# Half of the sums of halves in FFN2's seven-product multiplication made by GpSimd instead of VectorE

## The chip, the cores and the metric

The kernel runs on one core of one Trainium2 chip. The metric is the device time of one execution in microseconds (us); lower is better. The core's engines are TensorE (PE in the profile; PEld is its weight load), VectorE (DVE), ScalarE (ACT), GpSimd (POOL) and SyncE (SP). Each runs its own instructions in order, and they wait for one another by semaphores.

## What is computed

Attention without softmax, then a two-layer feed-forward net whose activation has a learned slope for negative values. The core of the reference:

```python
# q, k, v: [8 batches, 12 heads, 448, 64];  d_model = 768, d_ff = 2048
scores = (1 / sqrt(64)) * q @ k.T
attn   = maximum(scores, 0) ** 2 / 448
x      = (attn @ v)                      # -> [8 * 448 = 3584 tokens, 768]
h      = x @ w_in                        # FFN1
g      = maximum(h, 0) + alpha * minimum(h, 0)
out    = g @ w_out                       # FFN2
```

## The kernel before

**Work and order.** Attention goes by quads: a quad is four heads of one batch, 24 quads in all, each in seven chunks (j = 0 to 6). A chunk is four score products on TensorE (L206), a relu that empties their two PSUM banks to `rl` (L215 on ScalarE or L217 on VectorE), and a square to `at` (L226 or L228). When a quad's seven chunks are there, 28 products with `vraw` (L237) make its part of x, and two copies (L249, L251) take that to `xT`. FFN1 goes by batch and by blocks `ff` of 128 hidden features, 16 of them: six matmuls (L303) into one bank, then ScalarE makes `neg` = relu(-h) (L310, L653) and VectorE makes `gT` from it and the bank (L311, L659, L541). FFN2 takes 128 tokens at a time, 28 tiles.

The order on every engine is written out by hand, as strings of words that `Walk` (P[0] to P[3]) and `Line` (P[4]) read. Instructions of one engine stand in its queue in the order of these words. A word `ca` or `cAAD` is chunks, `f` is a block of FFN1, `N` and `G` its `neg` and `gT`, `v` an attention output, `t` and `l` belong to the loads (below), and `+`, `*` and `-` to the pairs of FFN2.

**FFN2 by pairs.** Four tiles of tokens go one by one (L330); the other 24 go in 12 pairs, named a to l. A pair's two tiles and the two halves of the features give four blocks of g, a11 and a12 (first tile) and a21 and a22 (second); likewise w_out has four blocks, of which `w_mix` holds four mixtures (L356). Seven products of eight matmuls (L379) take the place of eight. For them `Pair.mix` makes four sums of halves of g, each 128 x 1024 in bf16:

```python
x, y, op = {1: (self.a21, self.a22, ALU.add),
            2: (self.s.get(1), self.a11, ALU.subtract),
            3: (self.a11, self.a21, ALU.subtract),
            4: (self.a12, self.s.get(2), ALU.subtract)}[i]
nc.vector.tensor_tensor(t, x, y, op)          # L415
```

The words for them end in a, b, c, d for sums 1, 2, 3, 4: `+aa` and `*ba` are sum 1 of pairs a and b. Sum 1 is read by sum 2 and by product 5; sum 2 by product 6 and by sum 4, which is written over it; sum 3 by product 7; sum 4 by product 3. Products 1, 2 and 4 read g itself. The outputs of the products are added up by L396 and L392 (`m`, `u`, `osb`) and stored by SyncE (L320). In the trace sums 1 and 3 read `S<-gT`, sum 2 `S<-S,gT`, sum 4 `S<-gT,S`. The tiles of S come from a pool of four.

**GpSimd's queue.** GpSimd issues the loads: q and k of a quad (L109), v (L116), and the weights. From quad 5 on, q and k are turned by a DMA transpose: a copy to `perm` (L188, L693) by VectorE or ScalarE, then SyncE's DMA_TRANSPOSE (L193) to `T`. Right after that stands `land` (L435), a copy of one element of `T` to `landed` on GpSimd, which so waits until the transpose has arrived; behind it stand the next quads' loads.

Of the kernel before, what the change touches and what calls it, by code (L numbers as in the profile page):

```python
# [20 lines left out]
def kernel(  # L21
# [10 lines left out]
    nc = tc.nc  # L32
# [113 lines left out]
    for lo, hi, eng in ((0, 4, nc.sync), (4, NJ, nc.scalar)):  # L146
        t = o_pool.tile([128, 2, (hi - lo) * D], F32, tag="o", name=f"qfirst{lo}")
# [141 lines left out]
    def may_read(t, halves=(0, 1)):  # L289
        for b in batches_of(*t):  # L290
            for h in halves:
                assert all((b, ff) in f1_done for ff in range(KF // 2 * h, KF // 2 * h + KF // 2)), "gT is not written"
# [65 lines left out]
    class Pair:  # L358
# [43 lines left out]
        def mix(self, *which):  # L402
            for i in which:
                for t, halves in {1: ((self.b, (0, 1)),), 2: ((self.a, (0,)),), 3: ((self.a, (0,)), (self.b, (0,))),
                                  4: ((self.a, (1,)),)}[i]:
                    may_read(t, halves)
                assert i != 4 or "6" in self.made
                self.made.append("abcd"[i - 1])
                t = self.s[2] if i == 4 else S_pool.tile([128, KH, 128], BF16, tag="S", name="S")
                self.s[i] = t  # L410
                x, y, op = {1: (self.a21, self.a22, ALU.add),
                            2: (self.s.get(1), self.a11, ALU.subtract),
                            3: (self.a11, self.a21, ALU.subtract),
                            4: (self.a12, self.s.get(2), ALU.subtract)}[i]
                nc.vector.tensor_tensor(t, x, y, op)  # L415

        def run(self, name):
            if name in "23":
# [392 lines left out]
```

## Time and profile before

| | us |
|---|---|
| median of 2 runs (lowest, highest) | 371.59 (371.26, 371.92) |
| the profiled execution, its own time | 371.61 |
| its span, first to last instruction | 369.5 |
| busy: TensorE / VectorE / ScalarE / GpSimd | 361.2 / 310.9 / 256.3 / 73.0 |
| VectorE's 48 sums (L415) | 32.8, 0.68 each |
| GpSimd's 18 landing copies: busy, and idle ahead of them | 4.8, 182.4 |

How to read it: a row of the list in order of time has a start and a length in us from the span's start, the engine, the line of the kernel, the operation, what it writes and reads, and how many; in brackets how long the engine was idle before it and what ended that. A row of stretches has its limits, its length and then the busy time of each engine with the number of instructions in brackets, the granted TensorE clock as a share of full speed, the share of the DMA engines, and GB/s. The profile counts the issue of a load (0.7 us) as busy time on GpSimd. TensorE's ends are modelled. GpSimd's spans are rough.

### The profile page before, as it was taken

What the parts mean: (1) busy time and instruction counts of PE and PEld (TensorE: products, weight loads), DVE (VectorE), ACT (ScalarE), POOL (GpSimd) and SP (SyncE); (2) the same over time, 40 slices, a digit from 0 to 9 for tenths busy, and PEclk for the clock granted to TensorE, in tenths of its full rate; (3) what the DMA queues carried; (4) which work ended last, traced back from release to release, by engine and by line L of the source; (5) the groups of instructions that cost most, each with busy time, mean ns of one, the idle gap of its engine ahead of it and who ended that gap; (6) DMA issues with size and microseconds to landing.
All of it is one profiled execution on the core that took longest, in us unless ns stands there. A gap on an engine that the chain in (4) does not pass through costs nothing.

```text
span 369.5 us, 8035 instructions
## 1 busy us (share of the span) xinstructions
PE 361.2 (98%) x3169; PEld 201.7 (55%) x3169; DVE 310.9 (84%) x513; ACT 256.3 (69%) x388; POOL 73.0 (20%) x120
## 2 busy tenths in 40 slices
PE   8799999999999999999999999999999999999995
PEld 6454564445454455445554555555555555778763
DVE  3989988885979989999989989898786869789873
ACT  5998676877998878888678778887754834344300
POOL 8567150304122222201231122020000000000000
PEclk9999999999999999999999999999999999999999
DMA  9999989998999858758796675882134110020125
GB/s 141 188 204 202 201 125 190 164 168 138 193 186 154 119 82 149 142 96 110 126 171 122 105 117 105 141 154 52 28 73 105 46 43 2 21 66 23 44 59 134
DMA packets 73398, 43.29 MB, mean 117 GB/s; under 512 B 40336, under 2 KB 72848, under 8 KB 73360
## 3 DMA queue, kind: packets, MB, share of 16 engines
q0 software_dynamic: 27136, 22.58, 41.9%
q1 hardware_dynamic: 45792, 19.81, 26.6%
q8 instruction: 24, 0.39, 0.4%
q10 hardware_dynamic: 432, 0.39, 0.4%
q14 instruction: 14, 0.11, 0.1%
HBM read 45.62 MB, written 11.01 MB: 153 GB/s over the span
## 4 chain that ended last, share of the span: by engine, by line
PE 89%; DVE 3%; ACT 3%; DMA 2%; issue 2%; SPq 1%; ACTq 0%; POOLq 0%
PE psum L303 32%; PE psum L379 28%; PE psum L206 9%; PE psum L237 9%; PE psum L330 6%; PE psum L501 4%; ACT rl L215 1%; DMA kraw<-in_k_dram 1%; DMA out_dram<-osb 1%; DVE gT L311 1%; ACT neg L310 1%; DVE w_mix L188 1%; PE psum L175 1%; SPq L320 1%; DVE T L178 0%
## 5 line engine op out<-in xcount | busy, mean ns | idle before, releaser
L303 PE MATMUL psum<-xT,w_in_sb 128*128 128x448 bf16 x672 | 134.5, 353 | 0.5 <-ACT xT L249 0.3
L215 ACT ACTIVATE rl<-psum 128x896 bf16<-128x896 f32 x114 | 100.9, 929 | 20.0 <-PE psum L206 15.9
L303 PEld LDWEIGHTS <-w_in_sb 128*128 128x128 bf16 x672 | 63.4, 98 | 65.2 <-issue 10.0
L217 DVE TENSOR_SCALAR rl<-psum 128x896 bf16<-128x896 f32 x54 | 58.5, 1086 | 11.3 <-PE psum L206 10.5
L228 DVE TENSOR_TENSOR at<-rl 128x896 bf16<-128x896 bf16 x105 | 61.9, 617 | 1.1 <-ACT rl L215 0.6
L653 ACT ACTIVATE neg<-psum 128x448 f32<-128x448 f32 x80 | 43.1, 547 | 23.7 <-PE psum L303 12.5
L659 DVE SCALAR_TENSOR_TENSOR gT<-neg,beta_sb,psum 128x448 bf16<-128x448 f32 x80 | 53.0, 676 | 7.6 <-ACT neg L653 6.4
L226 ACT ACTIVATE at<-rl 128x896 bf16<-128x896 bf16 x63 | 58.2, 954 | 0.1
L379 PEld LDWEIGHTS <-S 128*128 128x128 bf16 x384 | 36.7, 98 | 26.4 <-issue 3.4
L379 PE MATMUL psum<-w_mix,S 128*128 128x384 bf16 x288 | 51.0, 326 | 0.0
L206 PE MATMUL psum<-T 64*64 64x448 bf16 x672 | 46.5, 357 | 1.7 <-ACT rl L215 0.9
L435 POOL COPY landed<-T 1x1 bf16<-1x1 bf16 x18 | 4.8, 267 | 182.4 <-DMA T<-perm 158.8
L379 PEld LDWEIGHTS <-gT 128*128 128x128 bf16 x288 | 27.6, 98 | 20.0 <-issue 2.5
L237 PE MATMUL psum<-at,vraw 64*64 64x448 bf16 x672 | 36.2, 350 | 0.0
L379 PE MATMUL psum<-w_out_sb,gT 128*128 128x384 bf16 x192 | 34.9, 326 | 0.0
L396 DVE TENSOR_TENSOR osb<-psum,u 128x384 f32<-128x384 f32 x36 | 19.7, 553 | 12.0 <-PE psum L379 7.1
L206 PEld LDWEIGHTS <-T 64*64 64x64 bf16 x672 | 16.8, 105 | 23.1 <-issue 15.8
L237 PEld LDWEIGHTS <-vraw 64*64 64x64 bf16 x672 | 20.1, 107 | 12.5 <-issue 1.7
L311 DVE SCALAR_TENSOR_TENSOR gT<-neg,beta_sb,psum 128x448 bf16<-128x448 f32 x32 | 21.0, 677 | 3.9 <-ACT neg L310 3.3
L310 ACT ACTIVATE neg<-psum 128x448 f32<-128x448 f32 x32 | 17.2, 548 | 8.8 <-PE psum L303 6.1
L330 PE MATMUL psum<-w_out_sb,gT 128*128 128x512 bf16 (+1 forms) x128 | 22.0, 326 | 0.1
L249 ACT ACTIVATE xT<-psum 128x448 bf16<-128x448 f32 x28 | 15.5, 557 | 4.5 <-PE psum L237 4.5
(75 smaller groups left out, 339.3 us busy)
## 6 DMA issues: line engine op xcount, KB each, us to landing
out_dram<-osb SPq DMA_DIRECT2D x94, 96.0 KB, 2.2
vraw<-in_v_dram POOLq DMA_DIRECT2D x24, 224.0 KB, 6.3
qraw<-in_q_dram POOLq DMA_DIRECT2D x23, 224.0 KB, 4.1
kraw<-in_k_dram POOLq DMA_DIRECT2D x23, 224.0 KB, 5.9
w_in_sb<-in_moe_w_in_dram POOLq DMA_DIRECT2D x16, 192.0 KB, 7.9
w_out_sb<-in_moe_w_out_dram POOLq DMA_DIRECT2D x4, 512.0 KB, 10.1
w_out_sb<-in_moe_w_out_dram POOLq DMA_DIRECT2D x4, 256.0 KB, 8.6
out_dram<-osb SPq DMA_DIRECT2D x8, 128.0 KB, 2.9
```

Of the source, the lines that this page charges most:

```text
L206: nc.tensor.matmul(ps[64 * c:64 * c + 64, r, :S], t[64 * r:64 * r + 64, 1, j, 64 * c:64 * c + 64], t[64 * r:64 * r + 64, 0, :, 64 * c:64 * ...
L215: nc.scalar.activation(rl, ps[:, :, :S], ACTF.Relu)
L217: nc.vector.tensor_scalar(rl, ps[:, :, :S], 0.0, None, ALU.max)
L226: nc.scalar.activation(a, rl, ACTF.Square)
L228: nc.vector.tensor_tensor(a, rl, rl, ALU.mult)
L237: nc.tensor.matmul(ps[64 * s:64 * s + 64, r, :S], vv[64 * r:64 * r + 64, s, j, :], a[64 * r:64 * r + 64, s], start=(j == 0), stop=(j == NJ ...
L303: nc.tensor.matmul(ps, w_in_sb[:, km // 2, km % 2, bass.ts(ff, 128)], xT[b][:, km // 2, km % 2, :], start=(km == 0), stop=(km == KM - 1))
L311: nc.vector.scalar_tensor_tensor(gT[:, ff, (b % 2) * S:(b % 2) * S + S], neg, beta_sb[:, ff:ff + 1], ps, ALU.mult, ALU.add)
L330: nc.tensor.matmul(psum[:, i, :hi - lo], gT[:, ff, bass.ts(c, 128)], w_out_sb[:, ff, lo:hi], start=(ff == 0), stop=(ff == KF - 1))
L379: nc.tensor.matmul(ps, left[:, i], right[:, i], start=(start and i == 0), stop=(i == KH - 1), skip_group_check=not start)
L653: nc.scalar.activation(neg, ps, ACTF.Relu, scale=-1.0)
L659: nc.vector.scalar_tensor_tensor(gT[:, ff, (b % 2) * S:(b % 2) * S + S], neg, beta_sb[:, ff:ff + 1], ps, ALU.mult, ALU.add)
```

## The change

Sums 1 and 3 of every pair are made by GpSimd, sums 2 and 4 stay on VectorE. The words of the order are the same, so each of the 24 sums that move takes its place in GpSimd's queue by where its word stands:

```diff
                             2: (self.s.get(1), self.a11, ALU.subtract),
                             3: (self.a11, self.a21, ALU.subtract),
                             4: (self.a12, self.s.get(2), ALU.subtract)}[i]
-                nc.vector.tensor_tensor(t, x, y, op)
+                (nc.gpsimd if i in (1, 3) else nc.vector).tensor_tensor(t, x, y, op)
```

TensorE's and ScalarE's orders stay as they are. Sum 2 now waits for GpSimd's semaphore, and products 5 and 7 too.

GpSimd at the first pair (P[3], words `l9` to `l10`), after the change; before, the sums' row is not there and the rest reads the same. The first landing copy is that of quad 9, the second that of quad 10:

```order
L435 COPY landed<-T 1x1
L109 DMA qraw<-in_q_dram 128x2x448
L109 DMA kraw<-in_k_dram 128x2x448
L116 DMA vraw<-in_v_dram 128x2x448
L415 TENSOR_TENSOR S<-gT 128x1024 x2
L435 COPY landed<-T 1x1
```

Sums 1 and 3 of pair a stand behind quad 9's landing copy and the three loads that follow it.

VectorE at the same place, before:

```order
L356 TENSOR_TENSOR w_mix_101<-w_out_sb 128x1536
L415 TENSOR_TENSOR S<-gT 128x1024
L228 TENSOR_TENSOR at<-rl 128x896
L415 TENSOR_TENSOR S<-gT 128x1024
L415 TENSOR_TENSOR S<-S,gT 128x1024
L228 TENSOR_TENSOR at<-rl 128x896 x2
L356 TENSOR_TENSOR w_mix_101<-w_out_sb 128x1536
L217 TENSOR_SCALAR rl<-psum 128x896
```

and after:

```order
L356 TENSOR_TENSOR w_mix_101<-w_out_sb 128x1536
L228 TENSOR_TENSOR at<-rl 128x896
L415 TENSOR_TENSOR S<-S,gT 128x1024
L228 TENSOR_TENSOR at<-rl 128x896 x2
L356 TENSOR_TENSOR w_mix_101<-w_out_sb 128x1536
L217 TENSOR_SCALAR rl<-psum 128x896
```

Sum 2 keeps its place among the squares, the mixture of w_out and the relu; the two sums ahead of it are gone from this queue.

GpSimd from pair g to the end, after the change:

```order
L435 COPY landed<-T 1x1
L109 DMA qraw<-in_q_dram 128x2x448
L109 DMA kraw<-in_k_dram 128x2x448
L116 DMA vraw<-in_v_dram 128x2x448
L415 TENSOR_TENSOR S<-gT 128x1024 x2
L435 COPY landed<-T 1x1
L116 DMA vraw<-in_v_dram 128x2x448
L435 COPY landed<-T 1x1
L415 TENSOR_TENSOR S<-gT 128x1024 x10
```

Pair g's two sums stand behind the loads of a landing copy, and the ten sums of pairs h to l behind the last one, with nothing else on the queue. In pairs i and j sum 3 of each comes first, and in i to l sum 1 of one pair is followed by sum 1 of its partner.

## The prediction

> **What bounds the kernel now.** I read the page's busy shares and chain first, then TensorE by stretches of the span, then GpSimd, VectorE and TensorE in order of time around the first pair.
>
> ```profile
> PE 361.2 (98%) x3169; PEld 201.7 (55%) x3169; DVE 310.9 (84%) x513; ACT 256.3 (69%) x388; POOL 73.0 (20%) x120
> PE 89%; DVE 3%; ACT 3%; DMA 2%; issue 2%; SPq 1%; ACTq 0%; POOLq 0%
> 92.00:112.00 20.00, 19.75 (x195) 9.91 (x194) 17.40 (x29) 19.41 (x26) 4.52 (x7) 1.00 1.02 181
> 112.00:300.00 188.00, 187.94 (x1618) 98.51 (x1616) 165.59 (x260) 144.91 (x213) 28.95 (x50) 1.00 0.63 109
> 300.00:365.00 65.00, 65.00 (x465) 44.39 (x458) 53.88 (x104) 21.02 (x42) 0.00 (x0) 1.00 0.19 45
> ```
>
> The last three rows are stretches: length, then busy time of PE, PEld, DVE, ACT, POOL. TensorE sets the time: from 92 us, where the sums begin, to 365 it is idle for 0.25 + 0.06 + 0 = 0.3 us. Time taken off VectorE there can buy at most that 0.3, while whatever makes TensorE wait is added to the end. GpSimd's 20% is not free time in the sense that matters, since its queue is in order and spends its idle time inside one waiting instruction, as the next rows show.
>
> **The first pair.** GpSimd, VectorE and TensorE from 87 to 100 us (start, length, instruction):
>
> ```profile
> 87.56 0.75 POOL L116 DMA_DIRECT2D vraw<-in_v_dram  x1
> 99.45 0.84 POOL L435 COPY landed<-T 1x1 bf16<-1x1 bf16 x1 [11.14 <-DMA T<-perm]
> 100.24 0.72 POOL L109 DMA_DIRECT2D qraw<-in_q_dram  x1
> 101.71 0.72 POOL L109 DMA_DIRECT2D kraw<-in_k_dram  x1 [0.75 <-DVE xT L251]
> 102.42 0.72 POOL L116 DMA_DIRECT2D vraw<-in_v_dram  x1
> ```
> ```profile
> 93.37 0.68 DVE L415 TENSOR_TENSOR S<-gT 128x1024 bf16<-128x1024 bf16 x1
> ...
> 95.11 0.68 DVE L415 TENSOR_TENSOR S<-S,gT 128x1024 bf16<-128x1024 bf16 x1
> 95.71 1.28 DVE L228 TENSOR_TENSOR at<-rl 128x896 bf16<-128x896 bf16 x2
> 96.90 0.95 DVE L356 TENSOR_TENSOR w_mix<-w_out_sb 128x1536 bf16<-128x1536 bf16 x1
> 97.77 1.08 DVE L217 TENSOR_SCALAR rl<-psum 128x896 bf16<-128x896 f32 x1
> ...
> 99.31 0.95 DVE L356 TENSOR_TENSOR w_mix<-w_out_sb,w_mix 128x1536 bf16<-128x1536 bf16 x1
> ```
> ```profile
> 97.71 1.66 PE L237 MATMUL psum<-at,vraw 64*64 64x448 bf16 x28
> 99.03 0.72 PE L206 MATMUL psum<-T 64*64 64x448 bf16 x8
> ```
>
> In the changed order the pair's sums 1 and 3 stand on GpSimd behind this landing copy and its three loads. The copy waits for quad 9's transpose, which nothing in the change brings forward, so sum 1 cannot begin before the loads are issued: at 99.45 + 0.18 (the copy undisturbed, below) + 0.3 of issue + 3 x 0.72 = 102.1 at the earliest, at 103.14 if the copy stays long and the 0.75 gap before kraw stays. I take 102.5. Sum 2 (95.11 now) stays on VectorE and reads sum 1. Until it comes, everything behind it on VectorE waits: two squares, a w_mix half, the relu at 97.77.
>
> **What a sum costs on GpSimd.** No GpSimd instruction with two inputs is in the trace. The nearest rows:
>
> ```profile
> 0.31 0.10 POOL L795 MEMSET const-bfloat16-1.0<- 128x1 bf16 x1
> 2.07 0.22 POOL masks.py:197 MEMSET ident<- 128x128 bf16 x1
> 2.37 0.29 POOL masks.py:199 TENSOR_SCALAR_AFFINE_SELECT ident<-ident 128x128 bf16<-128x128 bf16 x1
> L415 DVE TENSOR_TENSOR S<-gT 128x1024 bf16<-128x1024 bf16 x24 | 16.4, 683 | 0.1
> ```
>
> A write costs (0.22 - 0.10) / 127 = 0.95 ns an element, one input raises it to (0.29 - 0.10) / 127 = 1.5. Two inputs, extrapolated: about 2.0 ns x 1024 + 0.10 = 2.1 us. Ends: 1.1 us (the write's slope alone) and 3.2 (two passes at the one-input slope). I take 2.1, as it is nearest to what the rows say of inputs.
>
> [...]
>
> **The terms**, against the profiled execution's own 371.61 us (span 369.5 and 2.1 around it), which stands 0.02 above the median of the runs.
>
> 1. *VectorE held at pair a: 9.1 us.* Sum 1 ends at 102.5 + 2.1 = 104.6, sum 2 starts at 104.65 in place of 95.11: VectorE is 9.5 late. TensorE first lacks a square of the two from 95.71 within the 28 matmuls from 97.71 on, then the bank that the relu (97.77 to 98.85) empties for the second half of the eight from 99.03, some 0.2 into them. So 0.4 of the 9.5 is slack: 9.1 on the path. Ends 7.6 (sum of 1.1 us, start at 102.1) and 10.8 (3.2 us, 103.1).
>
> 2. *TensorE's clock: 2.0 us.* It would sit idle from about 98.8 to 106. What idling does shows at the span's two ends:
>
> ```profile
> 1.06 4.13 PE L157 MATMUL psum<-idle 128*128 128x128 bf16 x37 [1.06 <-DVE idle L143]
> 10.71 0.62 PE L626 MATMUL psum<-idle 128*128 128x128 bf16 x8
> 363.91 1.46 PE L379 MATMUL psum<-w_out_sb,gT 128*128 128x384 bf16 x8
> 365.40:367.80 2.40, 0.00 (x0) 0.00 (x0) 0.00 (x0) 0.48 (x1) 0.00 (x0) 1.00 0.73 191
> 367.90:369.40 1.50, 0.00 (x0) 0.00 (x0) 0.00 (x0) 0.00 (x0) 0.00 (x0) 0.50 0.00 1
> ```
>
> The granted clock falls to 0.50 some 2.5 us after the last matmul (365.37). At the start the same matmul comes every (4.13 - 0.31) / 36 = 0.106 us for 3.8 us (0.31 is one's own length); at 10.7 us every (0.62 - 0.22) / 7 = 0.057. So after 7 idle us about 4 us run at half pace: 2.0 lost. Ends 0 (it stays up) and 3.
>
> 3. *Other sums that come late: 2.2 us.* The same reckoning for all 24, with GpSimd's loads and the inputs' times, leaves these places; the rest end before they are wanted.
>
> ```profile
> 242.53 0.73 POOL L116 DMA_DIRECT2D vraw<-in_v_dram  x1
> 243.59 0.68 DVE L415 TENSOR_TENSOR S<-S,gT 128x1024 bf16<-128x1024 bf16 x1
> 316.13 0.67 DVE L659 SCALAR_TENSOR_TENSOR gT<-neg,beta_sb,psum 128x448 bf16<-128x448 f32 x1
> 317.74 0.69 DVE L415 TENSOR_TENSOR S<-S,gT 128x1024 bf16<-128x1024 bf16 x1
> 318.81 1.17 PEld L379 LDWEIGHTS <-S 128*128 128x128 bf16 x8
> 348.86 1.26 DVE L541 SCALAR_TENSOR_TENSOR gT<-ng,beta_sb,psum 128x448 bf16<-128x448 f32 x2
> 350.89 0.69 DVE L415 TENSOR_TENSOR S<-S,gT 128x1024 bf16<-128x1024 bf16 x1
> 352.05 3.51 PEld L379 LDWEIGHTS <-S 128*128 128x128 bf16 x22
> ```
>
> Pair g: loads end at 243.26, sum 1 at 245.4, sum 2 wanted at 243.59: VectorE 1.8 late; its next works are F1 outputs, so I charge 0.5. Pair i: the last gT lands at 316.8, sum 1 ends at 318.9, sum 2 was to start at 317.74: 1.2 late, and product 6 loads sum 2 at 318.81, 0.38 after its end: 0.8. Pair k: gT at 350.1, sum 1 ends at 352.2 against 350.89: 1.35 late, product 6 loads it 0.47 after its end: 0.9. Ends 0.3 and 5.5.
>
> 4. *Collisions of GpSimd with VectorE: 3.7 us.*
>
> ```profile
> 110.09 0.18 POOL L435 COPY landed<-T 1x1 bf16<-1x1 bf16 x1 [6.95 <-DMA T<-perm]
> 176.72 0.68 DVE L415 TENSOR_TENSOR S<-gT,S 128x1024 bf16<-128x1024 bf16 x1
> 176.87 0.57 POOL L435 COPY landed<-T 1x1 bf16<-1x1 bf16 x1 [9.00 <-DMA T<-perm]
> ```
>
> A landing copy of one element takes 0.18 us. Those begun inside a VectorE instruction with two SBUF inputs last until it ends: 0.57 here (to 177.44 against 177.40), 0.84 at 99.45 (to 100.29, the w_mix above ends at 100.26). The other direction, VectorE held by a 2.1 us GpSimd sum, no row shows: between 0 and 2.1 each. It counts where a GpSimd sum follows at once behind the one that sum 2 awaits and so starts first: pairs a, b, g, i, k (sum 3, or the partner pair's sum 1). At half, about 1.0 each, less what slack is left: 1.0 + 0.2 + 0.7 + 0.9 + 0.9 = 3.7. Ends 0 and 9.
>
> [...]
>
> 5. *VectorE's relief: -0.3.* It loses 24 x 0.6 = 14 us of work, covered by the 0.3 that TensorE is idle.
>
> Moved past and left as it is: each later landing copy stands behind one or two sums, but waits 159 / 16 = 10 us for its transpose anyway, longer than two sums take, so the loads leave on time:
>
> ```profile
> POOL landed L435 <- DMA T<-perm: 158.8, 16, 16.1
> ```
>
> Sum: 9.1 + 2.0 + 2.2 + 3.7 - 0.3 = 16.7; 371.6 + 16.7 = **388.3 us**.
>
> **Rivals.** *Not slower, 371.3 us:* GpSimd makes sum 1 of pair a inside its idle stretch from 88.31 to 99.45 (its gT was ready then), so VectorE is not held and only the relief is left. It decides if the sum starts before about 92. For it: GpSimd idle for 11.14 us. Against it: the order, where the sum stands behind the waiting copy on the same queue. 0.03. *VectorE held for whole sums:* five collisions at full length, 2.1 + 1.0 + 1.8 + 2.1 + 2.1 = 9.1 in place of 3.7: 393.7. For it: the landing copies; against it, only that this direction is unseen. 0.27. *Everything cheap:* a sum of 1.1 us, no clock drop, no collision, 7.6 + 0.3: 379.5. It needs three things at once. 0.09. *A sum of 3.2 us or more:* 10.8 + 2.0 + 5.5 + 5: about 395, and more if it collides whole. 0.06. That the change does nothing is excluded: 24 instructions leave VectorE in the order.
>
> **How the numbers follow.** Forecast 0.55, rivals 0.27, 0.09, 0.06, 0.03. The range 380.5 to 397 leaves out the cheapest end, the longest collisions and the rival of no loss. Slower by over 2% (above 379.0; 2% is about what a measurement of this kernel can tell from no change) is every case but the last and a part of the cheap one: 0.95; within 0.04; faster 0.01.
>
> **What would show it.** Right: L415 on GpSimd x24 at some 2.1 us; its first start near 102.5; an idle VectorE of about 10 us before S<-S,gT at 105, a wait of TensorE on L228 and L217 there, a granted clock of 0.5 for about 4 us; small waits of PEld L379 in the last 60 us. Wrong: a GpSimd sum before 99 us, or a VectorE that goes on past its waiting sum; terms 2 and 4 are wrong if the clock stays at 1.00 or sum 2 starts the moment sum 1 ends while sum 3 runs.

## The result and the profile after

| | us |
|---|---|
| before | 371.59 |
| after, median of 2 runs (lowest, highest) | 405.6 (404.25, 406.95) |
| ratio, with its 95% interval | 1.0911 (1.0886 to 1.0937) |
| after, the profiled execution: its own time, its span | 406.95, 405.2 |

The forecast was 388.3 and its range ended at 397, so the kernel lost about twice what was foreseen. In some experiments below the profiled execution was the slowest of its kernel (whole reads, quarter sums, both remedies together), and three of ten executions of the run with writes took 612 to 2101 us: sizes are taken from the medians, the ratios leave these executions out, and what is read from such a profile holds for that execution.

The page of the kernel after, engines and granted clock:

```profile
PE 370.1 (91%) x3169; PEld 204.2 (50%) x3169; DVE 319.1 (79%) x489; ACT 256.7 (63%) x388; POOL 123.3 (30%) x144
...
PEclk9999999999689999999998999999999999899989
```

VectorE has 24 instructions fewer and is busy 8.2 us longer (319.1 against 310.9): that is the first sign that something else than waiting happens to it. The clock drops at four places, not at one. Its stretches at 0.50, and one between the first two, from the view of stretches (length, busy time of PE, PEld, DVE, ACT, POOL, then the clock):

```profile
103.94:114.18 10.24, 3.72 (x20) 1.55 (x20) 8.34 (x9) 2.77 (x4) 3.93 (x2) 0.50 0.33 47
216.58:219.99 3.41, 3.29 (x11) 1.27 (x10) 3.41 (x6) 2.62 (x4) 0.00 (x0) 0.50 0.25 59
349.70:353.11 3.41, 3.41 (x18) 2.43 (x16) 2.01 (x4) 0.59 (x2) 0.00 (x0) 0.50 0.00 0
387.24:390.65 3.41, 3.41 (x13) 1.57 (x12) 1.79 (x4) 0.00 (x0) 0.00 (x0) 0.50 0.24 58
114.18:216.58 102.40, 95.89 (x844) 49.56 (x842) 91.73 (x128) 76.99 (x114) 36.82 (x41) 1.00 0.71 118
```

The groups of VectorE that matter here, in the kernel before:

```profile
L228 DVE TENSOR_TENSOR at<-rl 128x896 bf16<-128x896 bf16 x105 | 61.9, 617 | 1.1 <-ACT rl L215 0.6
L659 DVE SCALAR_TENSOR_TENSOR gT<-neg,beta_sb,psum 128x448 bf16<-128x448 f32 x80 | 53.0, 676 | 7.6 <-ACT neg L653 6.4
L415 DVE TENSOR_TENSOR S<-S,gT 128x1024 bf16<-128x1024 bf16 x12 | 8.2, 684 | 0.1
L415 DVE TENSOR_TENSOR S<-gT,S 128x1024 bf16<-128x1024 bf16 x12 | 8.2, 682 | 0.0
```

and after, with GpSimd's sums:

```profile
L228 DVE TENSOR_TENSOR at<-rl 128x896 bf16<-128x896 bf16 x105 | 72.2, 717 | 1.7 <-ACT rl L215 1.2
L659 DVE SCALAR_TENSOR_TENSOR gT<-neg,beta_sb,psum 128x448 bf16<-128x448 f32 x80 | 52.9, 675 | 10.2 <-ACT neg L653 9.1
L415 DVE TENSOR_TENSOR S<-S,gT 128x1024 bf16<-128x1024 bf16 x12 | 18.1, 1508 | 20.0 <-POOL S L415 20.0
L415 DVE TENSOR_TENSOR S<-gT,S 128x1024 bf16<-128x1024 bf16 x12 | 9.6, 803 | 0.0
```
```profile
L415 POOL TENSOR_TENSOR S<-gT 128x1024 bf16<-128x1024 bf16 x24 | 51.2, 2152 | 72.7 <-DVE gT L659 39.5
```

A sum takes 2.15 us on GpSimd; the estimate was 2.1. VectorE's instructions with two inputs in SBUF (squares, sums 2, sums 4) grew by 10.3 + 9.9 + 1.4 = 21.6 us, while L659, which reads one of its inputs from PSUM, stayed (53.0 and 52.9). Besides, sum 2 waited 20.0 us for sum 1.

The first pair in order of time:

```profile
99.96 0.18 POOL L435 COPY landed<-T 1x1 bf16<-1x1 bf16 x1 [10.97 <-DMA T<-perm]
...
102.22 0.72 POOL L109 DMA_DIRECT2D kraw<-in_k_dram  x1 [1.02 <-issue]
102.93 0.72 POOL L116 DMA_DIRECT2D vraw<-in_v_dram  x1
103.67 4.20 POOL L415 TENSOR_TENSOR S<-gT 128x1024 bf16<-128x1024 bf16 x2
105.84 2.60 DVE L415 TENSOR_TENSOR S<-S,gT 128x1024 bf16<-128x1024 bf16 x1 [11.44 <-POOL S L415]
108.36 1.15 DVE L228 TENSOR_TENSOR at<-rl 128x896 bf16<-128x896 bf16 x2
109.02 0.59 PE L237 MATMUL psum<-at,vraw 64*64 64x448 bf16 x4 [9.43 <-DVE at L228]
```

The order is the one that the prediction gave: the copy, the loads, sum 1 (at 103.67, it took 102.5), then sum 2, whose 0.68 us became 2.60 while sum 3 ran until 107.87.

TensorE does the same matmuls in the same order in both kernels, so the start of one can be subtracted from the start of the same one. This gives how late TensorE is, and where it becomes late (times of before; the total is 35.7):

| place | what TensorE lacked | predicted | measured |
|---|---|---|---|
| pair a, 98.8 and 99.2 | a square, then a relu | 9.1 + 1.0 = 10.1 | 9.8 + 2.0 = 11.8 |
| pairs i and k, 318.9 and 352.2 | sum 2 | 1.7 + 1.8 = 3.5 | 2.9 + 2.8 = 5.7 |
| pair g, 247.6 and 250.4 | a relu, then gT | 0.5 + 0.7 = 1.2 | 2.1 + 1.3 = 3.4 |
| pairs b, c, d, e, f | work that stands on VectorE behind held squares or a sum 2 (relus, an output, a copy); at b a relu of ScalarE that waits for a held square | 0.2 | 1.7 + 1.9 + 0.7 + 2.8 + 1.0 = 8.1 |
| half clock | | 2.0 | 1.1 + 3 x 1.7 = 6.2 |
| relief | | -0.3 | not seen |

The rows of pairs b to f and of the half clock carry most of the miss: 8.1 us where 0.2 was given, 6.2 where 2.0 was. The rows add up to 35.2; TensorE is 0.4 late already at 92, and the rest is rounding.

Pair c shows what term 3's words "the rest end before they are wanted" left out. Its sums are wanted later, but one of them runs beside a square:

```profile
158.67 0.73 POOL L116 DMA_DIRECT2D vraw<-in_v_dram  x1
...
159.32 2.73 DVE L228 TENSOR_TENSOR at<-rl 128x896 bf16<-128x896 bf16 x1
...
159.40 2.16 POOL L415 TENSOR_TENSOR S<-gT 128x1024 bf16<-128x1024 bf16 x1
...
161.98 1.08 DVE L217 TENSOR_SCALAR rl<-psum 128x896 bf16<-128x896 f32 x1
```

The square lasts until 162.05, 0.49 behind the sum's end, and the relu behind it on VectorE ends at 163.06; TensorE waits for that and loses 1.9. At pair e the loss is larger, since both of the pair's sums follow each other:

```profile
209.33 0.73 POOL L116 DMA_DIRECT2D vraw<-in_v_dram  x1
209.52 5.79 DVE L228 TENSOR_TENSOR at<-rl 128x896 bf16<-128x896 bf16 x2 [1.06 <-ACT rl L215]
210.06 4.23 POOL L415 TENSOR_TENSOR S<-gT 128x1024 bf16<-128x1024 bf16 x2
```

The two squares (1.15 us for two at 108.36) end 1.02 after the second sum: neither came through before it ended.

### The profile page after: what moved, and what is told of

It reads as the page before. It is cut to its first block, busy times and chain, and to the rows that moved or that the text cites. A ratio compares the mean times of both kernels' runs of the same rounds, so it can differ in the third digit from the quotient of the medians.

```text
span 405.2 us, 8043 instructions
## 1 busy us (share of the span) xinstructions
PE 370.1 (91%) x3169; PEld 204.2 (50%) x3169; DVE 319.1 (79%) x489; ACT 256.7 (63%) x388; POOL 123.3 (30%) x144
## 5 line engine op out<-in xcount | busy, mean ns | idle before, releaser
L303 PE MATMUL psum<-xT,w_in_sb 128*128 128x448 bf16 x672 | 136.1, 355 | 5.2 <-ACT rl L215 2.0
L228 DVE TENSOR_TENSOR at<-rl 128x896 bf16<-128x896 bf16 x105 | 72.2, 717 | 1.7 <-ACT rl L215 1.2
L415 POOL TENSOR_TENSOR S<-gT 128x1024 bf16<-128x1024 bf16 x24 | 51.2, 2152 | 72.7 <-DVE gT L659 39.5
L659 DVE SCALAR_TENSOR_TENSOR gT<-neg,beta_sb,psum 128x448 bf16<-128x448 f32 x80 | 52.9, 675 | 10.2 <-ACT neg L653 9.1
L379 PE MATMUL psum<-w_mix,S 128*128 128x384 bf16 x288 | 54.4, 341 | 5.3 <-DVE S L415 5.3
L206 PE MATMUL psum<-T 64*64 64x448 bf16 x672 | 48.7, 360 | 7.7 <-DVE rl L217 3.6
L435 POOL COPY landed<-T 1x1 bf16<-1x1 bf16 x18 | 3.6, 198 | 170.8 <-DMA T<-perm 133.7
L379 PEld LDWEIGHTS <-S 128*128 128x128 bf16 x384 | 37.8, 101 | 34.3 <-issue 6.6
L415 DVE TENSOR_TENSOR S<-S,gT 128x1024 bf16<-128x1024 bf16 x12 | 18.1, 1508 | 20.0 <-POOL S L415 20.0
## 6 DMA issues: line engine op xcount, KB each, us to landing
w_out_sb<-in_moe_w_out_dram POOLq DMA_DIRECT2D x4, 512.0 KB, 10.6
```

The source lines that it names most:

```text
L206: nc.tensor.matmul(ps[64 * c:64 * c + 64, r, :S], t[64 * r:64 * r + 64, 1, j, 64 * c:64 * c + 64], t[64 * r:64 * r + 64, 0, :, 64 * c:64 * ...
L228: nc.vector.tensor_tensor(a, rl, rl, ALU.mult)
L303: nc.tensor.matmul(ps, w_in_sb[:, km // 2, km % 2, bass.ts(ff, 128)], xT[b][:, km // 2, km % 2, :], start=(km == 0), stop=(km == KM - 1))
L379: nc.tensor.matmul(ps, left[:, i], right[:, i], start=(start and i == 0), stop=(i == KH - 1), skip_group_check=not start)
L415: (nc.gpsimd if i in (1, 3) else nc.vector).tensor_tensor(t, x, y, op)
L659: nc.vector.scalar_tensor_tensor(gT[:, ff, (b % 2) * S:(b % 2) * S + S], neg, beta_sb[:, ff:ff + 1], ps, ALU.mult, ALU.add)
```

## The experiments

Two theories were tested. *Exclusion:* while GpSimd reads SBUF for a sum, a VectorE instruction with two SBUF inputs stands still until the sum's end, wherever it is (sum 2 at pair a: 2.60 us in place of 0.68), and this makes most of the loss outside pair a. *Waits:* the loss is sum 2 and the products waiting for sums that come late, and what stands beside them costs nothing. All ratios are to the kernel before on the same chip, with the 95% interval.

### Pair a alone

```diff
-nc.vector.tensor_tensor(t, x, y, op)
+(nc.gpsimd if i in (1, 3) and self.a == (0, 3) else nc.vector).tensor_tensor(t, x, y, op)
```

> Only pair a's sums 1 and 3 go to GpSimd, the other 22 stay on VectorE. In the changed kernel TensorE's delay against before grows by 12.8 us at pair a (from 0.4 at 92 us to 13.2 at 112): 9.7 in the attention product, 2.0 at the relu behind sum 2, 1.0 at half clock. If these 12.8 belong to that place alone, 371.6 + 12.8 = 384.4 us, within 1.5. If instead VectorE without its relief catches up or loses elsewhere, it lies under 381 or over 388.

Measured: 385.49 us, 1.0377 (1.0360 to 1.0394). TensorE is 14.0 late at 112 and stays at that to the end. So pair a is worth 14 us by itself, and 20 of the 34 arise elsewhere, though the forecast had 4.6 there (16.7 less 12.1).

### Readers and writers on GpSimd that nothing waits for

VectorE makes all 48 sums as before; GpSimd repeats sums 1 and 3 into a scratch tile that nobody reads, in four pieces:

```diff
 nc.vector.tensor_tensor(t, x, y, op)
+if i in (1, 3):
+    for c in range(0, KH, 2):
+        nc.gpsimd.tensor_tensor(scratch, x[:, c:c + 2], y[:, c:c + 2], op)
```

> All 48 sums stay on VectorE. GpSimd makes sums 1 and 3 a second time, at the same places of its queue, in four pieces of 256 columns, and throws them away into a small scratch tile. Nothing waits for them. Theory of exclusion (a VectorE instruction with two SBUF inputs can't run while GpSimd reads SBUF, and is held to the end of GpSimd's work): the squares and sums of VectorE still get held, so 380 to 392 us and squares (L228 in the rows of before) above 650 ns on the mean. Theory of waits (all the loss comes from work that waits for a sum that is late): 371 to 373.5 us, squares at 617 ns.

Measured: 374.2 us, 1.0086 (1.0064 to 1.0109). The squares took 654 ns on the mean, as exclusion had it, but the time lies between the two theories. In place of the readers, writers:

```diff
+if i in (1, 3):
+    for c in range(6):
+        nc.gpsimd.memset(scratch, 1.0)
```

> All 48 sums stay on VectorE. GpSimd fills a scratch tile instead, six memsets of 256 columns at each of the same 24 places, about as long (6 x 0.35 = 2.1 us), without reading SBUF. If only reads of GpSimd exclude VectorE's two-input instructions: 371 to 373 us, squares at 617 ns. If any GpSimd instruction does: as the run with extra reads, 380 or more. Theory of waits: 371 to 373.

Measured: 371.54 us, 0.9996 (0.9986 to 1.0006). Groups of the writers' kernel (first fence) and of the readers' (second):

```profile
L419 POOL MEMSET scratch<- 128x256 bf16 x144 | 45.1, 313 | 7.6
L229 DVE TENSOR_TENSOR at<-rl 128x896 bf16<-128x896 bf16 x105 | 62.0, 618 | 1.1 <-ACT rl L216 0.6
L416 DVE TENSOR_TENSOR S<-gT 128x1024 bf16<-128x1024 bf16 x24 | 16.4, 684 | 0.1
```
```profile
L419 POOL TENSOR_TENSOR scratch<-gT 128x256 bf16<-128x256 bf16 x96 | 76.1, 793 | 60.1 <-DVE gT L663 31.8 <-DVE gT L545 22.2
L229 DVE TENSOR_TENSOR at<-rl 128x896 bf16<-128x896 bf16 x105 | 65.7, 654 | 1.0 <-ACT rl L216 0.6
L416 DVE TENSOR_TENSOR S<-gT 128x1024 bf16<-128x1024 bf16 x24 | 18.8, 783 | 0.1
```

45 us of writes leave VectorE's sums at 684 ns and its squares at 618; 76 us of reads lengthen them to 783 and 654. In these two runs it is the reading that holds. Whether the small loss came from the short pieces was then asked with whole ones. To make room for a scratch tile of 1024 columns, the outputs got five buffers instead of six, and a kernel with only that is the control:

```diff
-    o_pool = ctx.enter_context(tc.tile_pool(name="o", bufs=6))
+    o_pool = ctx.enter_context(tc.tile_pool(name="o", bufs=5))
 ...
+if i in (1, 3):
+    nc.gpsimd.tensor_tensor(scratch, x, y, op)
```

> As the run with extra reads, but each thrown-away GpSimd sum is one instruction of 1024 columns, as in the changed kernel (to make room for the scratch tile, the pool of output tiles has five buffers in place of six). No instruction waits for these sums; VectorE makes all 48 itself. Theory of exclusion: VectorE is held for whole GpSimd sums, squares near 700 ns on the mean, 382 to 391 us. Theory of waits: 371 to 373.

> The kernel before with five output buffers in place of six, the control for the run with whole extra reads: 371 to 372.5 us by both theories.

Measured: whole reads 405.0 us, 1.0879 (1.0827 to 1.0931); the control 371.38, 0.9992 (0.9979 to 1.0005). With no wait of VectorE or TensorE for GpSimd in its trace, this kernel is as slow as the changed one. That is above what even exclusion was expected to cost (382 to 391): VectorE here has 24 more instructions that can be held, its own sums 1 and 3; besides, in the profiled execution, the slowest, the clock fell to 0.50 at seven places. These 24 took 1391 ns each in place of 683:

```profile
L418 POOL TENSOR_TENSOR scratch<-gT 128x1024 bf16<-128x1024 bf16 x24 | 54.5, 2271 | 74.7 <-DVE gT L662 43.4 <-DVE gT L544 30.6
L416 DVE TENSOR_TENSOR S<-gT 128x1024 bf16<-128x1024 bf16 x24 | 33.4, 1391 | 0.1
```

The waits theory falls with this run, as an account of everything outside pair a.

### One of the two sums

```diff
+(nc.gpsimd if i == 3 else nc.vector).tensor_tensor(t, x, y, op)
```

> Only sums 3 go to GpSimd; no sum 2 waits then. Theory of waits: only product 7 waits, at pair a for 103.1 + 2.1 = 105.3 against 101.0, so 4.3 us, and nothing elsewhere: 376 us. Theory of exclusion: besides that the squares, sums 2 and mixtures that meet a sum 3: 379 to 386.

Measured: 383.04 us, 1.0311 (1.0264 to 1.0358), as exclusion expected. Its trace has one wait of TensorE for GpSimd, at pair a, where product 7 reads sum 3:

```profile
PE psum L379 <- POOL S L415: 4.2, 1, 4.2
```

The other 7 us are a half clock behind that wait (1.7) and the pairs d to g, 1.0 to 2.0 at each.

```diff
+(nc.gpsimd if i == 1 else nc.vector).tensor_tensor(t, x, y, op)
```

> Only sums 1 go to GpSimd. Sum 2 still waits at pair a (10.3 us, 12 with half clock) and at g, i and k (1 to 2 each), but no sum 3 follows behind sum 1 that holds sum 2. By exclusion: 386 to 393 us, and S<-S,gT at 0.7 to 1.0 us on the mean in place of 1.5. If sum 1's wait were the whole of the loss: 403 to 406.

Measured: 395.08 us, 1.0619 (1.0588 to 1.0649), 2 above the expected band. It had taken pairs i and k for free of holds without sum 3. But there the sum that follows at once is sum 1 of the partner pair, and sum 2 was held for 2.59 as before; TensorE lost 2.9 and 2.8 there ahead of the half clock, the same as with the whole change.

### Pair a's sums ahead of the loads

The words `+aa +ac` are moved ahead of `l9`, so that GpSimd makes these sums before it waits for quad 9's transpose:

```diff
-... g011 w10 l9 s0D Lq11 Lv9 s0D cA w20 +aa s1D cAA +ac s0A +ab s0D
+... g011 w10 +aa +ac l9 s0D Lq11 Lv9 s0D cA w20 s1D cAA s0A +ab s0D
```

> The changed kernel with pair a's two sums ahead of quad 9's landing copy on GpSimd's queue, so they can run from 89 us. Sum 2 finds sum 1 made. If pair a's loss is that of the queue's order, 12.8 of it goes, less what the sums now hold of VectorE at 89 to 93 us (two mixtures and squares, about 1 to 2 on TensorE): 393 to 395 us. If the loss there is the price of the sums on GpSimd wherever they stand, 401 or more.

Measured: 398.62 us, 1.0743 (1.0688 to 1.0797). Pair a then costs 1.3 in place of 12.9, so the wait there is that of the queue's order. But only 7 us come back: at pair b TensorE loses 5.9, a wait of 4.4 and a drop of the clock, in place of 1.7. The likely reason is that in the changed kernel TensorE came to pair b 13 us late, with work of VectorE done ahead; this was not tried by itself.

### Shorter instructions

Each sum on GpSimd as four instructions of 256 columns:

```diff
+if i in (1, 3):
+    for c in range(0, KH, 2):
+        nc.gpsimd.tensor_tensor(t[:, c:c + 2], x[:, c:c + 2], y[:, c:c + 2], op)
+else:
+    nc.vector.tensor_tensor(t, x, y, op)
```

> The changed kernel with each GpSimd sum in four instructions of 256 columns (four times 0.1 us of fixed cost, so 0.3 longer in all). If VectorE is held for one GpSimd instruction and gets in between two: a hold is at most about 0.65 us in place of 2.1, the collisions shrink to a third, and of the 35 us some 10 to 12 go: 393 to 397 us. If VectorE is held to the end of all GpSimd work that follows back to back (as two squares were, 5.79 us over two sums): no gain, 406 to 410. Theory of waits: 406 to 408, as each sum is 0.3 longer.

Measured: 396.5 us, 1.0627 (1.0547 to 1.0706): 9 us less than with whole sums, as expected if VectorE can come in between two pieces. In the trace nearly all of it arises at pairs i and k, where TensorE lost 0.0 and 0.6 in place of 4.6 and 4.5 (half clock included). Two things changed there. Sum 2 took 1.14 in place of 2.59; and the pieces of sum 1 start before all of their input is there, so that at pair i sum 2 began 0.78 after the last gT, in place of 2.33. The 9 us are therefore not the price of the long holds alone. Nor does VectorE always come in. At pair e the second of the same two squares waits for seven of the eight pieces and ends at 214.56:

```profile
208.82 5.74 DVE L228 TENSOR_TENSOR at<-rl 128x896 bf16<-128x896 bf16 x2 [1.05 <-ACT rl L215]
```
```profile
209.66 5.43 POOL L417 TENSOR_TENSOR S<-gT 128x256 bf16<-128x256 bf16 x8
```

Both remedies together:

> Both remedies together: each GpSimd sum in four instructions, and pair a's ahead of the landing copy. If the wait at pair a (e1: 14 us) and the holds elsewhere are separate losses, this has neither: 396.5 - 14 + 1 to 3 = 383 to 386 us. If the holds take the place of the wait, 390 or more.

Measured: 382.33 us, 1.0257 (1.0218 to 1.0297). By the medians the earlier sums bring back 14 us with short pieces, as much as pair a cost, where they brought 7 with long ones. That pair b was spared here is not shown: in the profiled execution (389.25 us) it took 5.0, with a drop of the clock. The kernel is still 10.6 us slower than before on the same chip.

### The clock

Ahead of product 6 of pairs i and k, 40 matmuls on a tile that is not otherwise used, into the bank that the product then overwrites:

```diff
+if name == "6" and self.a in ((2, 6), (3, 3)):
+    for _ in range(40):
+        nc.tensor.matmul(ps[:, :128], idle, idle, start=True, stop=True)
```

> The changed kernel with 40 idle matmuls (2.3 us at full clock) ahead of product 6 of pairs i and k, where TensorE waits 2.7 and 2.6 us for sum 2 and then runs 3.41 us at half clock. If the half clock follows from the idle time, both stretches vanish and 2 x 1.7 = 3.4 us go: 402.0 to 402.8 us. If it has another cause, nothing goes: 405 to 407.

Measured: 402.6 us, 1.0823 (1.0797 to 1.0849), 3.0 less than with the whole change. At pair i, the kernel after (first fence) and this one (second):

```profile
345.26 0.45 PE L501 MATMUL psum<-ts,w_in_sb 128*128 128x224 bf16 x3
348.42 1.54 PE L379 MATMUL psum<-w_mix,S 128*128 128x384 bf16 x8 [2.71 <-DVE S L415]
349.75 0.77 PE L501 MATMUL psum<-xT,w_in_sb 128*128 128x224 bf16 x3
```
```profile
344.36 2.40 PE L380 MATMUL psum<-idle 128*128 128x128 bf16 x40
347.24 1.47 PE L382 MATMUL psum<-w_mix,S 128*128 128x384 bf16 x8 [0.48 <-DVE S L418]
348.55 0.45 PE L504 MATMUL psum<-xT,w_in_sb 128*128 128x224 bf16 x3
```

The product still waits for sum 2, but the three matmuls behind it take 0.45, not 0.77. The half clock behind a stall is a cost of its own. That it is gone is read from the trace; the 3.0 is less certain, as the two runs of the kernel after lie 2.7 apart.

### The relief

Sum 3 on GpSimd only at pairs c, k and l, where no VectorE instruction with two SBUF inputs stands beside it:

```diff
+(nc.gpsimd if i == 3 and self.a in ((1, 0), (3, 3), (3, 5)) else nc.vector).tensor_tensor(t, x, y, op)
```

> Only the sums 3 of pairs c, k and l go to GpSimd: three that in the trace of before would run while VectorE has no instruction with two SBUF inputs, and that product 7 wants much later. 3 x 0.6 = 1.8 us of VectorE's work are gone, nothing is held. If VectorE's relief is worth nothing because TensorE sets the time: 371.0 to 372.0 us, no difference. If relief shortens the kernel, 369.8. If a sum on GpSimd costs something wherever it stands, 373 or more.

Measured: 371.51 us, 1.0003 (0.9979 to 1.0027). Three sums leave VectorE, nothing is held (squares at 618 ns, the sums that stay at 683 to 686), and nothing is won. No way of dividing the sums that was tried beats the kernel before.

## Why the prediction was wrong in its size

**What held.** TensorE sets the time, and VectorE's relief is worth nothing (0.3 given, none seen in the last run above: 371.51 us against 371.78). Sum 1 stands behind the landing copy: VectorE idle for 11.44 us ahead of its sum 2, where "about 10" was to be seen. Terms 1 and 2 and the share of term 4 at pair a made 12.1; TensorE lost 12.9 there, and was 14.0 late behind it in the run with pair a alone. That these are so near is in part luck: the hold was put 1.7 too low (10.1 against 11.8) and the half clock 0.9 too high (2.0 against 1.1). The GpSimd sum is 2.15. That pairs g, i and k pay as well was right. The gap ahead of kraw's issue (1.02) stayed though VectorE was idle; what it waits for is open.

**The step that failed: term 4.** "The other direction, VectorE held by a 2.1 us GpSimd sum, no row shows: between 0 and 2.1 each", then "At half, about 1.0 each", and only "where a GpSimd sum follows at once behind the one that sum 2 awaits". Both halves were wrong.

- The length. VectorE is held to the end of the sum: 1.9 over its own 0.68 at pairs a, g, i and k (2.60, 2.60, 2.59, 2.59). At i and k the rival of whole sums has 0.8 + 2.1 and 0.9 + 2.1, against 2.9 and 2.8 measured: there it is right within 0.2.
- The places. The prediction left the squares out. Of the ten VectorE instructions in the trace that are longer than their kind by over 1 us, four are or begin a group of squares (b, c, e, f), five are sums 2 (a, d, g, i, k), and one is a sum 4, beside pair h's sums. Those at b to f made TensorE 8.1 us late, where the prediction had 0.2. The rival of whole sums, with the same five places, ended at 393.7 and so missed as well.

The evidence was in the trace of before: the landing copies were held to the end of VectorE's instruction (0.57 and 0.84 us in place of 0.18), and the starts of the squares stood beside the times of the sums that were worked out for term 3. To take half of the range between 0 and 2.1 for want of a row, when the only row on the pair of engines showed a hold to the end, was the choice that went wrong.

The runs bear out a hold as long as the sum, for GpSimd instructions that read: beside a sum, sum 2 took 2.60 us in place of 0.68, while 144 memsets, which read nothing from SBUF, left the squares at 618 ns and the kernel at 371.54 us. Which of two instructions goes first is less clear from the recorded starts, below.

**Term 2 was mis-sized.** It counted one drop of the clock, 2.0; there are four, 1.1 + 3 x 1.7 = 6.2. The stalls at i and k (2.71 and 2.64) and that at e (two jumps of 2.2 and 0.6 close together) were followed by one, those of 1.7 to 2.1 at b, c and g were not; the last section shows that the length of a stall alone does not decide it. The prediction did not ask this of its own late sums at i and k, which it made shorter than they are. The run with 40 matmuls in the stall returned 3.0 of the 3.4 that two of these cost.

**Term 3** has no error of its own at i and k (it gave 0.8 and 0.9; 1.0 and 0.9 are left of 2.9 and 2.8 without the hold of 1.9). At g it gave 0.5; with the hold TensorE lost 3.4, in which the two are not told apart.

## What to carry to other kernels

Before work goes to GpSimd, look at what stands ahead of it on that queue (here a copy that GpSimd waited 10.97 us to begin), and lay each reading instruction of GpSimd over VectorE's: in this kernel VectorE's instructions with two SBUF inputs that met one were late by up to its whole length (a square at pair c took 2.73 us in place of 0.62; at pair e two, beside two sums in a row, 5.79 in place of 1.15), so it is VectorE's neighbours that are to be counted, not only the readers of the result. Where TensorE was idle for no more than 0.3 us between 92 and 365, time taken off VectorE bought nothing (371.51 us against 371.78), and stalls of 2.71 and 2.64 us were paid a second time in a slower clock, at 1.7 us each. A missing price that one row bears on from the other side is better taken from that row than from the middle.

## What the runs showed of the hardware that was not expected

**The one recorded first is not always first.** The squares at 159.32 and 209.52 began 0.08 and 0.54 before the GpSimd sum and were still held to its end. Common to these places is that VectorE's instruction began beside the issue of the load that stands directly ahead of the sum. In the kernel with pair a's sums early, it began 0.05 before that issue and 0.78 before the sum, longer than it takes (0.68):

```profile
188.06 3.50 DVE L415 TENSOR_TENSOR S<-S,gT 128x1024 bf16<-128x1024 bf16 x1
188.11 0.73 POOL L116 DMA_DIRECT2D vraw<-in_v_dram  x1
...
188.84 2.16 POOL L415 TENSOR_TENSOR S<-gT 128x1024 bf16<-128x1024 bf16 x1
```

Issues alone do not hold it (before, 105 squares at 617 ns among all the loads). Either the hold begins with the issue ahead of the sum, or GpSimd's recorded starts are late there; no run tells these apart.

**Two in a row.** At pairs b and e of the kernel after, VectorE did not come in between two sums that followed without a gap (three squares in 3.98 us, two in 5.79); at pair h it did (sum 4 in 2.14), and the second sum took 2.56. In the whole-reads kernel, whose successive GpSimd sums stand 0.08 apart, no VectorE instruction was held beyond the end of one sum (two squares ended at 119.18, beside two sums from 116.53 to 121.15). With a gap it came in each time, without one sometimes (pair h, and pairs i and k of the kernel with quarter sums); what decides then is open, and the gap was not tried by itself.

**The clock's steps.** The stretches at 0.50 are 3.41, 3.41, 3.41 and 10.24 = 3 x 3.41 us long, and those at full clock between them, 102.40, 129.71 and 34.13, are 30, 38 and 10 times as long: in this trace all changes from the first drop on lie on one grid of 3.41 us. Waits of less than one step, 2.71 and 2.64, were followed by a drop.

How long TensorE is idle within one step of that grid tells the drops from the rest at the places looked at. In the kernel after it was idle for 2.25, 2.14 and 2.37 of the 3.41 us ahead of the drops at e, i and k, and for 1.80 and 1.70 in the fullest steps at b and g, where none followed. In the kernel with pair a's sums early the stall at pair i was 2.71 long too, but lay across two steps, and no drop followed. The step of pair i in the kernel after (first fence), then the stall and its longer step in the other (second):

```profile
346.28:349.70 3.42, 1.28 (x8) 0.80 (x9) 2.85 (x3) 0.00 (x0) 1.53 (x1) 1.00 0.24 58
```
```profile
341.74 1.48 PE L379 MATMUL psum<-w_mix,S 128*128 128x384 bf16 x8 [2.71 <-DVE S L415]
339.86:343.28 3.42, 1.54 (x11) 1.03 (x12) 2.59 (x3) 0.00 (x0) 1.27 (x1) 1.00 0.23 56
```

That is 3.42 - 1.28 = 2.14 idle with a drop, and 3.42 - 1.54 = 1.88 without. Since TensorE's ends are modelled, the limit between them is an estimate.
